# Head-pair loads and a folded row maximum at the start of a fused attention and feed-forward kernel

## The chip, the cores and the metric

One core of a Trainium2 chip. The metric is the device time of one execution in microseconds (us), median of several; the span in a profile, first to last instruction, is about 1.8 us shorter. Runs agree within some 0.5%, so a difference under 1 us in one pair of runs says little.

In the profiles PE is TensorE, PEld its weight loads, DVE VectorE, ACT ScalarE, POOL GpSimd and SPq SyncE's queue. SBUF is the core's on-chip memory; an eviction copies a matmul's result into SBUF; to issue a DMA is to hand it to the DMA engines, and it lands when its data has arrived.

## The reference, cut to what matters

Linear attention with random features (8 batches, 8 heads, 576 rows, 64 dimensions, 128 features), then a two-layer network (512 to 2048 to 512) on its 4608 rows:

```python
def phi(x):                        # x: q or k, scaled
    proj = np.einsum('bhsd,md->bhsm', x, omega)
    h = proj - np.sum(x * x, axis=-1, keepdims=True) / 2.0
    h = h - np.max(h, axis=-1, keepdims=True)      # row maximum over 128 features
    return np.exp(h) / np.sqrt(m)
kv  = np.einsum('bhsm,bhsd->bhmd', k_p, v);  z = np.sum(k_p, axis=2)
num = np.einsum('bhsm,bhmd->bhsd', q_p, kv); den = ... z ... + 1e-06
# x = num/den, heads side by side;  h = x @ w_in;  g = h*clip(h+3,0,6)/6;  return g @ w_out
```

In k's features the square term cancels against the maximum. The kernel takes the exponential first and then divides by the row maximum of the result, which it folds into v.

## The kernel before

A small scheduler in the program orders instructions and picks engines from estimated costs. Only batch 0 and 1 matter here. Cut to the parts concerned (cuts marked with `# ...`):

```python
# batch 0: k, q, v: one head of two head pairs per DMA (256 KB)
for x, (m0, m1) in enumerate(halves):            # [(0, 2), (2, 4)]
    for hh in range(2):
        # ...
        rows = src[b, 2 * m0 + hh:2 * m1 - 1 + hh:2, first:first + MAIN, :]
        dma("%s%d%d" % (t, hh, x), d[:, m0:m1, hh, :], rows.rearrange(...), 131072 * (m1 - m0), ...)
# ... cast to bf16 (kb), TensorE transposes, eviction (kT), projection, exponential (kp); nine units u:
op("DVE", dvet(512), lambda E, u=u: E.reduce_max(
    mx[pb][:, 4 * u:4 * u + 4], kp[pb][:, 4 * u:4 * u + 4, :], axis=AX.X), ...)
# reciprocals cc = 1/mx, then v scaled by them, on GpSimd (POOL) or VectorE (DVE):
op(EV_V if b else V0, {"POOL": 0.62, "DVE": dvet(260)}, lambda E, ...: E.tensor_tensor(
    vcl[pb][p0:p0 + 64, :, ...], vl[pb][p0:p0 + 64, :, :], <cc broadcast>, ALU.mult), ...)   # leftover rows
op(EV_V if b else V0, {"POOL": 1.2, "DVE": dvet(512)}, lambda E: E.tensor_tensor(
    vcm[:, :, 0:D], v32[:, m, :, :], cbc, ALU.mult), ...)                                     # vc of pair m
# TensorE: kv product of pair m: eight 65-wide matmuls kp x vc and one kp x vcl
```

The four kv products of batch 0 are the gate: before them TensorE has little to do, after them it hardly waits again.

The softmax here doesn't subtract the row's maximum and nothing guards it: scores larger than these inputs give would overflow.

Of the kernel before, what the change touches and what calls it, by code (L numbers as in the profile page):

```python
# [5 lines left out]
BF16 = mybir.dt.bfloat16  # L6
# [5 lines left out]

URGENT = 0.8
FIT = 0.05
IDLE_UNTIL = 21.0
# [27 lines left out]
class Prog:  # L43
# [60 lines left out]
    def schedule(self):  # L104
# [68 lines left out]
        while len(order) < n:  # L173
            best = None
            for e, lst in engines.items():
                cand = []
                for o in lst:
                    s = slot_of(o) if o.alloc else (0.0, ())
                    if s is None:
                        continue  # L180
                    cand.append((max(free[e], ready(o), s[0]), o, s[1]))
                if not cand:
                    continue
                idle = [x for x in cand if x[1].name == "idle"]
                cand = [x for x in cand if x[1].name != "idle"]
                m = min([x[0] for x in cand] + [1e9])
                if idle and (not cand or idle[0][0] + (0.02 if idle[0][0] < 8.0 else idle[0][1].occ) <= m):
                    if idle[0][0] > IDLE_UNTIL:
                        if not cand:
                            continue  # L190
                    elif best is None or idle[0][0] < best[0]:
                        best = (idle[0][0], e, idle[0][1], idle[0][2])
                        continue
                    else:
                        continue
                if not cand:
                    continue
                c = min((x for x in cand if x[0] <= m + (URGENT if x[1].prio < -1.0 else 0.02)),
                        key=lambda x: (x[1].prio, x[1].seq))
                fits = [x for x in cand if x[0] + (x[1].occ[e] if isinstance(x[1].occ, dict) else x[1].occ) <= c[0] + FIT]  # L200
                if c[0] > m + 0.02 and fits:
                    c = min(fits, key=lambda x: (x[1].prio, x[1].seq))
                if best is None or c[0] < best[0]:
                    best = (c[0], e, c[1], c[2])
# [7 lines left out]
            o.eng = e  # L212
            occ = o.occ[e] if isinstance(o.occ, dict) else o.occ
            for vx, i in zip(o.alloc, picks):
                old = vx.ring.held[i]
                if old is not None:
                    for d in old.users:
                        o.deps.setdefault(d, False)
                vx.slot = i
                vx.ring.held[i] = vx  # L220
# [98 lines left out]
def _emit(nc, es, q, k, v, omega, w_in, w_out, out):  # L319
# [13 lines left out]
    TU = [(0, 2), (2, 6), (6, 10), (10, 14), (14, 18)]  # L333
    HALVES = [(0, 2), (2, 4)]
    SPLIT = 3
    LATE = 0.4
    FIRST = [("k", 1), ("k", 0), ("q", 1), ("v", 0), ("v", 1), ("q", 0)]
    REST = [("k", 1), ("k", 0), ("q", 1), ("q", 0), ("v", 0), ("v", 1)]
    W_GATE = [("vl", 0)]*2+[("v32", 1, 3)]*2
    alpha = float(D) ** -0.25  # L340
    PE_T, PE_X = 2, 2
    SPARE = 1
    IDLE = (16, 60)
    EV_T = ("DVE", "ACT")
# [25 lines left out]
    kp = [sbt("kp%d" % u, [128, NCH, M], BF16) for u in range(2)]  # L370
    mx = [sbt("mx%d" % u, [128, NCH], F32) for u in range(2)]
    cc = [sbt("cc%d" % u, [128, NCH], F32) for u in range(2)]
    vc = [sbt("vc%d" % u, [128, 520], BF16) for u in range(2)]
# [34 lines left out]
    def dvet(n):  # L408
        return 0.07 + n / 960.0
# [64 lines left out]
    def w_in_piece(i, gate):  # L474
        f0, f1 = WI[i]
        op("POOL", 0.72 * (f1 - f0), lambda E: E.dma_start(
            wi[:, :, 128 * f0:128 * f1], w_in[:, 128 * f0:128 * f1].rearrange("(c p) f -> p c f", p=128)),
# [3 lines left out]
    def w_out_piece(g, gate):  # L481
        op("POOL", 2.95, lambda E: E.dma_start(
            wo[:, 4 * g:4 * g + 4, :], w_out[512 * g:512 * g + 512, :].rearrange("(c p) e -> p c e", p=128)),
# [7 lines left out]
    def load(b, eng, gates):  # L491
        pb = b % 2
        halves = HALVES if b == 0 else [(0, NP)]
        turn_of = [0]

        def dma(part, dst, src, n, keys, gate, prio, run):
            cast = b > 0 and part[0] in "kq"
            e = "POOL" if cast else eng[turn_of[0]] if turn_of[0] < len(eng) else "SP"
            op(e, n * (0.74 if b == 0 else 0.8) * (1.0 if run == 1024 else 1.5) / 262144.0,
               lambda E: E.dma_start(dst, src), prio + 0.001 * turn_of[0], reads=gate + (free if cast else []), writes=keys,  # L500
# [15 lines left out]
        def mains(t, src, dst):  # L516
            for x, (m0, m1) in enumerate(halves):
                for hh in range(2):
                    first = 64 * hh if t != "q" else 0
                    d = dst[:].rearrange("p m (h r) d -> p m h (r d)", h=2) if t == "v" else mains_of(dst)  # L520
                    rows = src[b, 2 * m0 + hh:2 * m1 - 1 + hh:2, first:first + MAIN, :]
                    dma("%s%d%d" % (t, hh, x), d[:, m0:m1, hh, :], rows.rearrange("m (p r) d -> p m (r d)", r=4),
                        131072 * (m1 - m0), landing(t, hh, m0, m1), gates[t], base[t], 1024)

# [20 lines left out]
    def attention(b):  # L545
# [19 lines left out]

        def four(m0, m1, hh):
            return [2 + 4 * m + 2 * hh + s for m in range(m0, m1) for s in range(2)]

        def every(m0, m1, s):
# [20 lines left out]

        def dbls(t):
            return t[:, 2:, :].rearrange("p (m h s) t -> p m h (s t)", h=2, s=2)

        def alts(t, s, m0, m1):
# [8 lines left out]
        if b == 0:  # L603
            for m0, m1 in HALVES:
                for hh in range(2):
                    nm = "%d%d" % (m0 // 2, hh)
                    dbl = four(m0, m1, hh)
                    cast("k", nm, 512, mains_of(kb)[:, m0:m1, hh, :], mains_of(k32)[:, m0:m1, hh, :],
                         main_keys("k", range(m0, m1), [hh]), dbl, 0)
                    turns("k", nm, dbl, dbls(kT)[:, m0:m1, hh, :], kb, 0)  # L610
            for s in range(2):
# [22 lines left out]
        for u in range(NU):  # L634
            vK = Virt(ring)

            def e_K(E, u=u, vK=vK):
# [9 lines left out]
               pos(u) + 0.02, reads=[vK], writes=[("kp", pb, u)], name="eK%d.%d" % (b, u))  # L647
            op("DVE", dvet(512), lambda E, u=u: E.reduce_max(  # L648
                mx[pb][:, 4 * u:4 * u + 4], kp[pb][:, 4 * u:4 * u + 4, :], axis=AX.X),
               pos(u) + 0.03, reads=[("kp", pb, u)], writes=[("mx", pb, u)], name="mx%d.%d" % (b, u))  # L650

# [25 lines left out]
        for hh in range(2):  # L677
            p0 = 64 * hh
            op(EV_V if b else V0, {"POOL": 0.62, "DVE": dvet(260)}, lambda E, hh=hh, p0=p0: E.tensor_tensor(  # L679
                vcl[pb][p0:p0 + 64, :, 65 * hh:65 * hh + 65], vl[pb][p0:p0 + 64, :, :],  # L680
# [57 lines left out]
    def pair(b, m, t):  # L738
# [10 lines left out]
        vcm = vc[u2][:].rearrange("p (c e) -> p c e", e=65)  # L749
        op(EV_V if b else V0, {"POOL": 1.2, "DVE": dvet(512)}, lambda E: E.tensor_tensor(  # L750
            vcm[:, :, 0:D], v32[:, m, :, :], cbc, ALU.mult),
# [263 lines left out]
```

## Time and profile before

| | before |
|---|---|
| time, median | 323.59 us (323.52 to 324.55) |
| span of the profiled run | 321.8 us |
| last kv product of batch 0 | 17.61 us |
| first second-layer matmul | 39.98 us |

```profile
12.33 1.43 POOL L679 TENSOR_TENSOR vcl<-vl,cc 64x260 bf16<-64x260 f32 x2
16.20 1.36 POOL L750 TENSOR_TENSOR vc<-v,cc 128x512 bf16<-128x512 f32 x1
```

While GpSimd multiplies vcl, VectorE does maxima; they last as long as elsewhere (five take 3.05 us in a row). While GpSimd multiplies vc, VectorE is already in its own vc, which it began 0.34 us sooner; VectorE's takes 0.80 us (its two others 0.70 and 0.69), GpSimd's 1.36, beside a median of 1.05 over its 22.

### The profile page before, as it was taken

The page shows a single profiled execution, that of the slowest core. Times are in us where ns is not written, and L with a number is a line of the kernel's source. Part 1 is how long each engine was busy: PE and PEld are TensorE (multiplying, and loading weights), DVE is VectorE, ACT ScalarE, POOL GpSimd, SP SyncE. Part 2 cuts the span into 40 slices and gives each one's busy share as a digit, 9 for nine tenths or more (in the row PEclk, how much of TensorE's full clock was granted, in tenths as well). Part 3 has the DMA queues.
Part 4 walks back from the last instruction along what each step waited for, and adds up shares of the span by engine and source line. Part 5 has one row for each costly group of instructions (what it writes and reads, how often), then busy time and mean ns, then how long its engine had stood idle before and what let it go on. Part 6 is the DMA issues. An engine that isn't in the chain of part 4 may idle for free.

```text
span 321.8 us, 5873 instructions
## 1 busy us (share of the span) xinstructions
PE 317.0 (98%) x2236; PEld 174.8 (54%) x2236; DVE 209.0 (65%) x460; ACT 189.1 (59%) x385; POOL 76.8 (24%) x107
## 2 busy tenths in 40 slices
PE   8999999999999999999999999999999999999996
PEld 6789855455654544565555545555555444444443
DVE  4988985597787947995796478846866353433411
ACT  3996982596595516966775387647674254344400
POOL 2765171065040600730333022402020000000000
DMA  7999999999940999897829963998012201000024
GB/s 249 269 201 204 236 146 234 225 184 170 226 122 34 136 173 271 99 196 118 236 31 188 191 208 39 183 201 224 16 50 67 73 27 41 33 35 33 33 67 98
DMA packets 91532, 44.79 MB, mean 139 GB/s; under 512 B 58096, under 2 KB 87024, under 8 KB 91504
## 3 DMA queue, kind: packets, MB, share of 16 engines
q1 hardware_dynamic: 64288, 31.31, 42.1%
q0 software_dynamic: 26512, 12.46, 31.4%
q10 hardware_dynamic: 704, 0.66, 0.6%
q8 instruction: 18, 0.29, 0.4%
q14 instruction: 10, 0.08, 0.1%
HBM read 36.73 MB, written 9.44 MB: 143 GB/s over the span
## 4 chain that ended last, share of the span: by engine, by line
PE 94%; DVE 4%; POOL 1%; issue 0%; ACT 0%; POOLq 0%; DVEq 0%
PE p L917 39%; PE p L859 34%; PE p L656 5%; PE p L639 4%; PE p L884 4%; PE p L791 3%; PE p L763 2%; DVE mx L648 2%; PE p L466 2%; PE p L429 1%; PE p L765 1%; POOL vc L750 0%; DVE vc L750 0%; DVE vcl L679 0%; DVE gT L895 0%
## 5 line engine op out<-in xcount | busy, mean ns | idle before, releaser
L917 PE MATMUL p<-wo,gT 128*128 128x512 bf16 (+2 forms) x592 | 141.0, 373 | 0.3 <-DVE qT L418 0.3
L867 DVE SCALAR_TENSOR_TENSOR gT<-tsb,p 128x512 bf16<-128x512 bf16 x128 | 86.8, 685 | 56.7 <-ACT tsb L865 56.1
L865 ACT ACTIVATE tsb<-p 128x512 bf16<-128x512 f32 x128 | 76.3, 601 | 71.1 <-PE p L859 70.6
L859 PE MATMUL p<-xT,wi 128*128 128x512 bf16 x448 | 107.3, 379 | 0.0
L917 PEld LDWEIGHTS p<-wo,gT 128*128 128x128 bf16 x592 | 56.1, 98 | 57.5 <-DVE qT L418 0.5
L859 PEld LDWEIGHTS p<-xT,wi 128*128 128x128 bf16 x448 | 42.6, 98 | 45.4
L648 DVE TENSOR_REDUCE mx<-kp 128x4 f32<-128x512 bf16 x72 | 46.7, 674 | 9.7 <-ACT kp L645 9.4
L645 ACT ACTIVATE kp<-p 128x512 bf16<-128x512 f32 x72 | 40.0, 619 | 15.1 <-PE p L639 15.1
L660 ACT ACTIVATE qpT<-p 128x512 bf16<-128x512 f32 (+1 forms) x80 | 41.4, 575 | 4.8 <-PE p L656 4.6
L750 POOL TENSOR_TENSOR vc<-v,cc 128x512 bf16<-128x512 f32 x22 | 23.4, 1064 | 36.3 <-DVE cc L746 27.0
L807 DVE TENSOR_TENSOR xb<-p,rec 128x384 bf16<-128x384 f32 (+1 forms) x64 | 28.5, 477 | 0.0
L639 PE MATMUL p<-om,kT 128*128 128x256 bf16 x144 | 23.0, 273 | 0.0
L656 PE MATMUL p<-qT,om 128*128 128x512 bf16 (+1 forms) x80 | 22.8, 358 | 0.0
L418 DVE COPY osb<-p 128x512 f32<-128x512 f32 (+2 forms) x12 | 7.8, 647 | 22.7 <-PE p L917 22.7
L417 ACT COPY osb<-p 128x512 f32<-128x512 f32 x25 | 14.8, 591 | 11.3 <-PE p L917 11.3
L500 POOL DMA_DIRECT2D k<-in_k_dram x12 | 9.1, 767 | 41.9 <-PE p L859 33.7
L639 PEld LDWEIGHTS p<-om,kT 128*128 128x128 bf16 x144 | 13.8, 98 | 9.7
L791 PEld LDWEIGHTS p<-kvz,qpT 128*128 128x128 bf16 x312 | 13.5, 98 | 5.8 <-ACT qpT L660 0.2
L859 PE MATMUL p<-xS,wi 128*128 128x512 bf16 x64 | 16.4, 379 | 0.0
L884 PE MATMUL p<-xT,wi 128*128 128x256 bf16 x128 | 15.9, 272 | 0.0
L763 PEld LDWEIGHTS p<-vc,kp 128*128 128x128 bf16 x256 | 11.9, 98 | 6.1 <-POOL vc L750 0.4
L791 PE MATMUL p<-kvz,qpT 128*128 128x65 bf16 x312 | 14.8, 194 | 0.0
(69 smaller groups left out, 215.9 us busy)
## 6 DMA issues: line engine op xcount, KB each, us to landing
out_dram<-osb SPq DMA_DIRECT2D x32, 256.0 KB, 2.6
v<-in_v_dram SPq DMA_DIRECT2D x14, 512.0 KB, 5.3
wi<-in_moe_w_in_dram POOLq DMA_DIRECT2D x4, 512.0 KB, 8.3
k<-in_k_dram POOLq DMA_DIRECT2D x8, 256.0 KB, 5.1
k<-in_q_dram POOLq DMA_DIRECT2D x8, 256.0 KB, 6.2
wo<-in_moe_w_out_dram POOLq DMA_DIRECT2D x4, 512.0 KB, 12.8
kb<-in_k_dram POOLq DMA_DIRECT2D x6, 256.0 KB, 5.3
qb<-in_q_dram POOLq DMA_DIRECT2D x6, 256.0 KB, 7.6
```

What stands on the lines that cost most here:

```text
L639: ins = E.matmul(ring.t[vK.slot][:, 256 * i:256 * i + 256], kT[:, 2 * u + i, :], om[:].rearrange("d t m -> d (t m)"), start=True, stop=True)
L645: op("ACT", actt(512), lambda E, u=u, vK=vK: E.activation(kp[pb][:, 4 * u:4 * u + 4, :].rearrange("p c m -> p (c m)"), ring.t[vK.slot], AF ...
L648: op("DVE", dvet(512), lambda E, u=u: E.reduce_max(mx[pb][:, 4 * u:4 * u + 4], kp[pb][:, 4 * u:4 * u + 4, :], axis=AX.X), pos(u) + 0.03, r ...
L656: op("PE", mmt(n), lambda E, vQ=vQ, lh=lh: E.matmul(ring.t[vQ.slot][:, 0:n], om[:, lh, :], src, start=True, stop=True), p + 0.045 * lh, re ...
L660: op("ACT", actt(n), lambda E, vQ=vQ, lh=lh: E.activation(dst(lh), ring.t[vQ.slot][:, 0:n].rearrange("m (j t) -> m j t", t=128), AF.Exp, s ...
L791: ins = E.matmul(d[:, hh, i - i0, :], qpT[pb][:, o:o + 128], kvz[m][:, 65 * hh:65 * hh + 65], start=True, stop=True)
L807: op("DVE", dvet(128 * n), lambda E: E.tensor_tensor(xv(i0, i1), psum()[:, :, :, 0:64], rbc, ALU.mult), t + 0.01, reads=[vn, ("rec", ru)], ...
L859: ins = E.matmul(ring.t[vh.slot], wi[:, c, 128 * f:128 * f + 128], xv[:, c, :], start=(c == 0), stop=(c == NJ - 1))
L865: op("ACT", actt(512), lambda E: E.activation(tsb[tu][:], ring.t[vh.slot], AF.Relu, bias=0.5, scale=1.0 / 6.0), t - 0.1, reads=[vh], write ...
L867: op("DVE", dvet(512), lambda E: E.scalar_tensor_tensor(gT[gu][:, f, :], tsb[tu][:], 1.0, ring.t[vh.slot], ALU.min, ALU.mult), t - 0.1, re ...
L884: ins = E.matmul(ring.t[vh.slot][:, 256 * g:256 * g + 256], wi[:, c, 128 * (f + g):128 * (f + g) + 128], xT[0][:, c, 256 * half:256 * half ...
L917: ins = E.matmul(ring.t[vo.slot][:, 0:c1 - c0], gT[gu][:, f, 128 * tc:128 * tc + 128], wo[:, f, c0:c1], start=(f == 0), stop=(f == NF - 1))
```

## The change

It is meant to bring the first bytes of k in sooner, so that the first batch's chain starts sooner, and to shorten the row maximum: a bf16 elementwise maximum of the features' two halves (the fold), then a maximum over 64. Scheduler constants and costs are adjusted with it, so order and engines change too. The core of the diff (cut):

```diff
-URGENT = 0.8
-FIT = 0.05
+COLD = 6.0
+URGENT = 0.5
+FIT = 0.1
...
+    PARTS = {"k": [(0, 1, 0, 1), (0, 1, 1, 2)] + [(1, 2, 0, 1), (1, 2, 1, 2)] + [(m, m + 1, 0, 2) for m in range(2, NP)],
+             "q": [(0, 2, 0, 1), (0, 2, 1, 2), (2, 4, 0, 1), (2, 4, 1, 2)],
+             "v": [(m, m + 1, 0, 2) for m in range(NP)]}
...
-    W_GATE = [("vl", 0)]*2+[("v32", 1, 3)]*2
+    W_GATE = [("q32", 1, 3)] * 2 + [("v32", 0, 1)] * 2
+    FOLD = 2
...
-            op("DVE", dvet(512), lambda E, u=u: E.reduce_max(
-                mx[pb][:, 4 * u:4 * u + 4], kp[pb][:, 4 * u:4 * u + 4, :], axis=AX.X),
+            if b >= FOLD:
+                ...                                     # as before
+            op("DVE", 0.07 + 256 / 1920.0, lambda E, u=u, fu=fu: E.tensor_tensor(
+                fold[fu][:], kp[pb][:, 4 * u:4 * u + 4, 0:64], kp[pb][:, 4 * u:4 * u + 4, 64:128], ALU.max), ...)
+            op("DVE", dvet(256), lambda E, u=u, fu=fu: E.reduce_max(
+                mx[pb][:, 4 * u:4 * u + 4], fold[fu][:], axis=AX.X), ...)
...
-        op(EV_V if b else V0, {"POOL": 1.2, "DVE": dvet(512)}, lambda E: E.tensor_tensor(
+        op(EV_V if b else V0, {"POOL": 1.32, "DVE": dvet(512)}, lambda E: E.tensor_tensor(
```

k's main rows now come in six DMAs (four of 128 KB, two of 256 KB) in place of four, with the leftover rows in one more.

More of the change, by code (lines that the diff above doesn't have):

```diff
@@ L186, in schedule @@
                 m = min([x[0] for x in cand] + [1e9])
-                if idle and (not cand or idle[0][0] + (0.02 if idle[0][0] < 8.0 else idle[0][1].occ) <= m):
+                if idle and (not cand or idle[0][0] + (0.02 if idle[0][0] < 4.8 else 0.2 if idle[0][0] < 8.0 else idle[0][1].occ) <= m):
                     if idle[0][0] > IDLE_UNTIL:
@@ L213, in schedule @@
             occ = o.occ[e] if isinstance(o.occ, dict) else o.occ
+            if e == "PE" and 4.0 < st < COLD:
+                occ *= 2.0
             for vx, i in zip(o.alloc, picks):
@@ L334, in _emit @@
     HALVES = [(0, 2), (2, 4)]
+    PARTS = {"k": [(0, 1, 0, 1), (0, 1, 1, 2)] + [(1, 2, 0, 1), (1, 2, 1, 2)] + [(m, m + 1, 0, 2) for m in range(2, NP)],
+             "q": [(0, 2, 0, 1), (0, 2, 1, 2), (2, 4, 0, 1), (2, 4, 1, 2)],
+             "v": [(m, m + 1, 0, 2) for m in range(NP)]}
+    KPARTS = [(m, h0, h1) for m, _, h0, h1 in PARTS["k"]]
     SPLIT = 3
@@ L371, in _emit @@
     mx = [sbt("mx%d" % u, [128, NCH], F32) for u in range(2)]
+    fold = [sbt("fold%d" % u, [128, 4, 64], BF16) for u in range(3)]
     cc = [sbt("cc%d" % u, [128, NCH], F32) for u in range(2)]
@@ L475, in w_in_piece @@
         f0, f1 = WI[i]
-        op("POOL", 0.72 * (f1 - f0), lambda E: E.dma_start(
+        op("POOL", 0.64 * (f1 - f0), lambda E: E.dma_start(
             wi[:, :, 128 * f0:128 * f1], w_in[:, 128 * f0:128 * f1].rearrange("(c p) f -> p c f", p=128)),
@@ L481, in w_out_piece @@
     def w_out_piece(g, gate):
-        op("POOL", 2.95, lambda E: E.dma_start(
+        op("POOL", 2.56, lambda E: E.dma_start(
             wo[:, 4 * g:4 * g + 4, :], w_out[512 * g:512 * g + 512, :].rearrange("(c p) e -> p c e", p=128)),
@@ L492, in load @@
         pb = b % 2
-        halves = HALVES if b == 0 else [(0, NP)]
         turn_of = [0]
@@ L498, in dma @@
             e = "POOL" if cast else eng[turn_of[0]] if turn_of[0] < len(eng) else "SP"
-            op(e, n * (0.74 if b == 0 else 0.8) * (1.0 if run == 1024 else 1.5) / 262144.0,
+            op(e, n * 0.74 * (1.0 if run == 1024 else 1.5) / 262144.0,
                lambda E: E.dma_start(dst, src), prio + 0.001 * turn_of[0], reads=gate + (free if cast else []), writes=keys,
@@ L516, in mains @@
         def mains(t, src, dst):
-            for x, (m0, m1) in enumerate(halves):
-                for hh in range(2):
-                    first = 64 * hh if t != "q" else 0
-                    d = dst[:].rearrange("p m (h r) d -> p m h (r d)", h=2) if t == "v" else mains_of(dst)
-                    rows = src[b, 2 * m0 + hh:2 * m1 - 1 + hh:2, first:first + MAIN, :]
-                    dma("%s%d%d" % (t, hh, x), d[:, m0:m1, hh, :], rows.rearrange("m (p r) d -> p m (r d)", r=4),
-                        131072 * (m1 - m0), landing(t, hh, m0, m1), gates[t], base[t], 1024)
+            for m0, m1, h0, h1 in PARTS[t] if b == 0 else [(0, NP, 0, 1), (0, NP, 1, 2)]:
+                off = 64 if t != "q" else 0
+                d = dst[:].rearrange("p m (h r) d -> p m h (r d)", h=2) if t == "v" else mains_of(dst)
+                rows = bass.AP(src.tensor, src.offset + ((b * H + 2 * m0 + h0) * S + off * h0) * D,
+                               [[4 * D, 128], [2 * S * D, m1 - m0], [(S + off) * D, h1 - h0], [1, 4 * D]])
+                dma("%s%d%d" % (t, m0, h0), d[:, m0:m1, h0:h1, :], rows, 131072 * (m1 - m0) * (h1 - h0),
+                    [x for hh in range(h0, h1) for x in landing(t, hh, m0, m1)], gates[t], base[t], 1024)
         def lefts_of(t, hh):
@@ L564, in rows_of @@
             return [k_ for x in dbl for k_ in ([(t + "b", pb, x, h) for h in hs] if x < 2 else [(t + "b", pb, x)])]
-        def four(m0, m1, hh):
-            return [2 + 4 * m + 2 * hh + s for m in range(m0, m1) for s in range(2)]
         def every(m0, m1, s):
@@ L589, in turns @@
                p, reads=[vT], writes=[(t + "T", x) for x in dbl], name="Tev%s%d.%s" % (t, b, name))
-        def dbls(t):
-            return t[:, 2:, :].rearrange("p (m h s) t -> p m h (s t)", h=2, s=2)
         def alts(t, s, m0, m1):
@@ L603, in attention @@
         if b == 0:
-            for m0, m1 in HALVES:
-                for hh in range(2):
-                    nm = "%d%d" % (m0 // 2, hh)
-                    dbl = four(m0, m1, hh)
-                    cast("k", nm, 512, mains_of(kb)[:, m0:m1, hh, :], mains_of(k32)[:, m0:m1, hh, :],
-                         main_keys("k", range(m0, m1), [hh]), dbl, 0)
-                    turns("k", nm, dbl, dbls(kT)[:, m0:m1, hh, :], kb, 0)
+            for m, h0, h1 in KPARTS:
+                nm = "%d%d" % (m, h0)
+                dbl = [2 + 4 * m + x for x in range(2 * h0, 2 * h1)]
+                cast("k", nm, 256 * (h1 - h0), mains_of(kb)[:, m, h0:h1, :], mains_of(k32)[:, m, h0:h1, :],
+                     main_keys("k", [m], range(h0, h1)), dbl, 0)
+                turns("k", nm, dbl, kT[:, dbl[0]:dbl[-1] + 1, :], kb, 0)
             for s in range(2):
@@ L647, in attention @@
                pos(u) + 0.02, reads=[vK], writes=[("kp", pb, u)], name="eK%d.%d" % (b, u))
-            op("DVE", dvet(512), lambda E, u=u: E.reduce_max(
-                mx[pb][:, 4 * u:4 * u + 4], kp[pb][:, 4 * u:4 * u + 4, :], axis=AX.X),
-               pos(u) + 0.03, reads=[("kp", pb, u)], writes=[("mx", pb, u)], name="mx%d.%d" % (b, u))
+            if b >= FOLD:
+                op("DVE", dvet(512), lambda E, u=u: E.reduce_max(
+                    mx[pb][:, 4 * u:4 * u + 4], kp[pb][:, 4 * u:4 * u + 4, :], axis=AX.X),
+                   pos(u) + 0.03, reads=[("kp", pb, u)], writes=[("mx", pb, u)], name="mx%d.%d" % (b, u))
+                continue
+            fu = u % 3
+            op("DVE", 0.07 + 256 / 1920.0, lambda E, u=u, fu=fu: E.tensor_tensor(
+                fold[fu][:], kp[pb][:, 4 * u:4 * u + 4, 0:64], kp[pb][:, 4 * u:4 * u + 4, 64:128], ALU.max),
+               pos(u) + 0.03, reads=[("kp", pb, u)], writes=[("fold", fu)], name="fold%d.%d" % (b, u))
+            op("DVE", dvet(256), lambda E, u=u, fu=fu: E.reduce_max(
+                mx[pb][:, 4 * u:4 * u + 4], fold[fu][:], axis=AX.X),
+               pos(u) + 0.03, reads=[("fold", fu)], writes=[("mx", pb, u)], name="mx%d.%d" % (b, u))
         def project(name, dbl, src, dst, p):
@@ L678, in attention @@
             p0 = 64 * hh
-            op(EV_V if b else V0, {"POOL": 0.62, "DVE": dvet(260)}, lambda E, hh=hh, p0=p0: E.tensor_tensor(
+            op(EV_V if b else V0, {"POOL": 0.72, "DVE": dvet(260)}, lambda E, hh=hh, p0=p0: E.tensor_tensor(
                 vcl[pb][p0:p0 + 64, :, 65 * hh:65 * hh + 65], vl[pb][p0:p0 + 64, :, :],
```

## The prediction

> **What bounds the kernel now.** I read the page first (busy shares, then the chain that ended last), then the chain in order of time for the first 45 us, then the timeline and busy time by stretch there, and last the waits.
>
> ```profile
> PE 317.0 (98%) x2236; PEld 174.8 (54%) x2236; DVE 209.0 (65%) x460; ACT 189.1 (59%) x385; POOL 76.8 (24%) x107
> ...
> PE 94%; DVE 4%; POOL 1%; issue 0%; ACT 0%; POOLq 0%; DVEq 0%
> ```
>
> TensorE carries 94% of the chain and is busy 98%. That busy share flatters it, since matmul ends are modelled, so I add up issue intervals instead. Runs of one form in the chain of waits give the interval: 42 matmuls of 256 columns in 4.59 us are 109 ns each, 40 of 512 columns in 8.63 us are 216 ns, and eight of 65 columns in 0.25 us are 31 ns. With the counts in the groups by form this makes 1136 x 216 ns = 245.0 us (512 columns), 288 x 109 = 31.4 (256), 576 x 31 = 17.9 (65), 120 transposes and the like at 56 = 6.7, and 4.4 for the 130 and 384 wide ones: 305.4 us of work that the change does not touch. The span is 321.8, so only 16.4 us are overhead. They are 1.3 us before the first matmul, about 3.0 after the last one (it ends near 318.8), 8.9 of filler matmuls, and 3.2 of true gaps. By stretch, the counts fill 60 to 290 us completely; the gaps lie in the first 40 us. There the chain is not TensorE alone:
>
> ```profile
> 1.32 2.74 PE p L466 x12
> ...
> 4.17 1.28 PE p L466 x6
> ...
> 8.05 0.65 DVE kT L418 x2
> 8.70 2.96 DVE mx L648 x5
> ...
> 11.91 0.68 DVE vc L750
> 12.59 1.19 DVE mx L648 x2
> 13.77 0.60 DVE vc L750
> 14.37 1.08 DVE mx L648 x2
> ...
> 16.20 1.37 POOL vc L750
> 17.57 0.05 issue
> 17.61 0.43 PE p L763 x8
> ```
>
> The columns are start, length and what. L466 is filler[...]. From 8.05 to 16.2 us VectorE paces the first batch: kT evictions, nine row maxima (L648), reciprocals and the scaling of v (vc). Then GpSimd scales the last v, and at 17.61 the last kv product goes out. From there on TensorE leads the chain, until batch 1 comes:
>
> ```profile
> 35.35 0.69 DVE gT L895
> 36.04 1.85 DVE mx L648 x4
> ...
> 38.62 0.87 DVE vcl L679
> ...
> 39.50 0.43 DVE qT L418
> ```
>
> Here TensorE truly waits again: of the 22.4 us from 17.6 to 40, counts times intervals account for 21.5, so 0.9 us is lost. These two places, the start and the 0.9 us, are all that the change can touch. The stretch view shows why arrival matters at the start:
>
> ```profile
> 2.00:4.00 2.00, 2.00 (x12) 1.44 (x11) 0.50 (x5) 1.22 (x2) 0.00 (x0) 1.00 0.94 319
> 4.00:6.00 2.00, 2.00 (x14) 1.51 (x13) 0.67 (x3) 1.06 (x2) 0.61 (x1) 1.00 1.04 315
> 10.00:12.00 2.00, 2.00 (x23) 1.69 (x21) 2.00 (x7) 2.00 (x6) 1.38 (x2) 1.00 1.11 347
> ```
>
> After stretch and length, the columns are busy time (count) of TensorE, its weight loads, VectorE, ScalarE and GpSimd, then clock, DMA share and GB/s. DMA is full from 2 us on; VectorE is idle until 6 us and full from 8 to 16.
>
> [...] 12 fillers in 2.74 us are 228 ns each, against 109 later. [...]
>
> **The change, part by part.**
>
> First loads. In the before kernel the first k casts start at 3.82 (ScalarE), 4.73 (GpSimd), 5.25 and 6.28 us, each on a 256 KB transfer that holds one head of two pairs. 256 KB at 320 GB/s is 0.82 us. After, the first four are 128 KB, so each lands about 0.4 us after its forerunner. I put the first pieces at 3.2 to 3.5 us, the fourth near 4.4, all of k near 6.3 as before (same bytes). The first exponential of k waited until 7.35 because four transposes of a whole 512-wide piece stood before it. In the built order of the changed kernel, eight transposes of 256-wide pieces and then the first projections stand there. VectorE's omega copies end at 4.79 as now; four 256-wide evictions at 0.28 us end at 5.9, so the exponentials can begin near 6. The later k pieces still gate the rest. Before its first fold VectorE also has the cast of the k leftovers (landing near 6.7, 0.28 us), a 512-wide eviction (0.42) and a 256-wide one (0.28), so it gets to the maxima at about 7.7 in place of 8.70: 1.0 us gained.
>
> Row maximum. For nine units: before 9 x 592 = 5.33 us. [...] The later batches keep the old maximum and lie where TensorE is full. [...]
>
> What moves. On VectorE one vc (about 0.65) goes to GpSimd, two vcl (64x260, about 0.33 each) come from GpSimd, and one qT eviction (0.42) comes from ScalarE: some 0.4 us more. Start 1.0 [...] - 0.4 = 1.2 us earlier at the last kv product, 16.4 in place of 17.61. GpSimd's second vc (1.37) could end a little later than that, but it starts sooner too, as the weight loads in front of it are issued sooner.
>
> TensorE order. Before the last kv product the changed kernel has six 512-wide q projections, the old one four: 2 x 216 ns = 0.43 us of work are pulled into the waiting time. Sum: 1.2 + 0.43 = 1.6 us.
>
> Cross-check by fillers. The built order has 52 in place of 63: three fewer at the cold rate (3 x 213 ns = 0.64) and eight fewer warm (8 x 109 = 0.87), 1.5 us less dead work. Two independent counts agree.
>
> Batch 1. [...] of the 0.9 us lost there I credit 0.2, since ScalarE is as full there (4.00 of 4 us between 36 and 40) and eight exponentials take 4.0 us. Against it: the loads of w_out do not hurry. DMA is full until 44 us and the first piece lands at 28.0 + 10.4 = 38.4, while the first second-layer matmul ran at 39.98; pulled forward by 1.6 it would meet the landing. I take 0.2 back. The new scheduling constants reorder later instructions too, but TensorE is full there: 0.
>
> Expected: 323.6 - 1.6 = 322.0 us, half a per cent.
>
> **The rivals.**
>
> A. The reorder only reveals another limit: DMA, full from 2 to 44 us. If v, the w_in pieces or w_out land when they landed before, TensorE waits on them and the gain shrinks to some 0.3 to 0.8 us (322.8 to 323.3). For it: the DMA share, and SyncE waiting 18.5 us on w_out. Against: the third and fourth w_out pieces now arrive 2 to 3 us before use, and w_in's gate moves from the v leftovers to a q piece that was issued earlier.
>
> B. The clock. Six early cold fillers become three, and the new rule for fillers leaves short gaps between 4.8 and 8 us unfilled. [...] 30 to 60 early matmuls run at half rate. That costs at most 3 us, but mostly inside time that waits for VectorE anyway; the result would be 322.5 to 325.
>
> C. More than I see: if VectorE's early idle time is really used up and batch 1's 0.9 us vanishes too, 2.5 to 3 us go, 320.6 to 321.
>
> D. A new stall mid-kernel from the changed scheduling (URGENT 0.5, FIT 0.1). One wait of a microsecond there would eat the gain, for TensorE has no slack there.
>
> **Range and chances.** The centre is 322.0. Four parts in five lie between C's best and a nearly lost gain, 320.8 to 323.3. Faster by 2% would need 6.5 us out of 16.4 of overhead, of which 4.3 are fixed ends and 7.4 are fillers that remain in the program's order: 1%. Slower by 2% needs 6.5 us of new waits, B and D together: 2%.
>
> **What would show it.** Right: the first exponential of k starts near 6 instead of 7.35; [...] the last of the four kv products is at 16 to 16.7; the filler group counts 52; the stretches from 60 to 290 us hold the same matmuls as before, only shifted by 1 to 2 us. Wrong: [...] matmuls of 256 columns at 213 ns after 6 us; a wait of TensorE on a DMA of w_in or w_out near 20 or 38 us; gaps between 60 and 300 us. If the kv product comes earlier but the first second-layer matmul still starts near 39.9, rival A holds.

What it said of the hardware without a measurement is cut, and with it what rested on that alone: the lengths of the fold and of the shorter maximum, and so the gain of the row maximum, one term of the sum. With that term the sum came to 1.2 us at the last kv product and to 1.6 us in all; the terms that are left, 1.0 and - 0.4, make 0.6 of the 1.2. The 592 ns of a maximum before come from its trace: five in a row take 2.96 us in the chain. The 0.33 of a vcl is an estimate: VectorE's shortest there is recorded with 426 ns, and a vc recorded with 0.69 us takes 0.60 in the chain. L466's fillers multiply constants while TensorE waits. The 512-wide matmuls of this trace are recorded with 379 ns on average, though they step by 216.

## More of the kernel before

In the timeline of SyncE's queue (start us, length us, engine, line, operation, tile, count) the line is a group of DMA issues; this is the time of issuing, not of transfer:

```profile
1.21 1.45 SPq L500 DMA_DIRECT2D k<-in_k_dram  x3
```

Three issues of k take 1.45 us, so k's last is out at 2.66. (ScalarE's queue issues two more of k meanwhile.) In the timelines of VectorE and of GpSimd, two pairs of lines overlap in time:

```profile
12.50 1.27 DVE L648 TENSOR_REDUCE mx<-kp 128x4 f32<-128x512 bf16 x2
15.86 0.80 DVE L750 TENSOR_TENSOR vc<-v,cc 128x512 bf16<-128x512 f32 x1
```

## The result, and the profile after

| | before | after |
|---|---|---|
| time, median (same rounds) | 323.77 us (323.52 to 325.13) | 324.58 us (324.02 to 325.29) |
| ratio | | 1.002, 95% interval 0.9996 to 1.0043 |
| span of the profiled run | 321.8 us | 322.6 us |
| first exponential of k | 7.35 us | 6.55 us |
| last kv product of batch 0 | 17.61 us | 19.32 us |
| first second-layer matmul | 39.98 us | 41.00 us |

A ratio here is the mean time of one kernel's fast runs over that of the other's in the same rounds, so it is not quite the ratio of the medians. No gain came, and the result is outside the predicted range. The traces show that the start became 1.7 us slower where 1.2 us were to be gained.

The page of the changed kernel, engines and chain:

```profile
PE 314.2 (97%) x2190; PEld 173.5 (54%) x2225; DVE 212.8 (66%) x489; ACT 187.5 (58%) x378; POOL 75.7 (23%) x107
...
PE 90%; DVE 4%; ACT 2%; DMA 1%; issue 1%; SPq 1%; DVEq 0%
```

TensorE's share of the chain fell from 94 to 90%. Its chain of waits at the start (start, length, what):

```profile
3.12 4.65 DMA k<-in_k_dram
...
7.80 0.38 DVE kb L427
...
8.84 0.40 DVE fold L655 x2
9.24 0.33 DVE mx L658
...
10.22 0.53 DVE fold L655
...
14.07 1.19 DVE vcl L689
...
15.70 0.80 DVE fold L655 x2
...
17.69 1.27 DVE vc L760
19.00 0.43 PE p L773 x8
```

Before, the chain up to 8 us was TensorE; now it hangs on a transfer of k until 7.77. The first two folds take 0.40 us, 0.20 each, but a single fold takes 0.53 at 10.22 and two take 0.80 at 15.70. The last vc takes 1.27 us, beside 0.60 and 0.68 for those of before. Two readings suggest themselves.

The first is in SyncE's queue:

```profile
1.20 2.39 SPq L508 DMA_DIRECT2D k<-in_k_dram  x5
```

Each issue takes 0.42 to 0.47 us, for 128 KB as for 256 KB. Two more of them put k's last issue 0.93 us later than before (3.59 beside 2.66), and the issues of q and v behind it wait as long. The windows tell the same by rate (after stretch and length: busy time and count of TensorE, weight loads, VectorE, ScalarE, GpSimd, then clock, DMA share, GB/s):

```profile
4.00:6.00 2.00, 2.00 (x16) 1.69 (x15) 1.59 (x6) 0.32 (x1) 0.64 (x3) 1.00 0.95 235
```

That is 235 GB/s in a stretch that had 315 before, although the DMA share is still 0.95. The last pair of k reaches its cast at 7.41 in place of 6.28.

The second is in the timelines of VectorE and GpSimd:

```profile
13.69 1.56 DVE L689 TENSOR_TENSOR vcl<-vl,cc 64x260 bf16<-64x260 f32 x2
15.62 0.89 DVE L655 TENSOR_TENSOR fold<-kp 128x256 bf16<-128x256 bf16 x2
17.60 1.34 DVE L760 TENSOR_TENSOR vc<-v,cc 128x512 bf16<-128x512 f32 x1
```

```profile
14.99 1.16 POOL L760 TENSOR_TENSOR vc<-v,cc 128x512 bf16<-128x512 f32 x1
17.35 1.05 POOL L760 TENSOR_TENSOR vc<-v,cc 128x512 bf16<-128x512 f32 x1 [1.20 <-DVE cc L756]
```

Each VectorE instruction that lasts too long reads two tiles of SBUF, and a GpSimd instruction lies beside it: its casts of q (9.32 to 10.61) beside the fold at 10.22, its vc beside the others (beside the vcl pair only for the last 0.26 us, by the records; before that GpSimd issues DMAs). The prediction had not reckoned with this. The vc product, the vcl product and the fold have two SBUF inputs. The maximum that the fold replaces has one, and in the kernel before it lasted as long beside GpSimd's vcl as elsewhere (two take 1.27 us at 12.50, beside it, and at 14.29).

So the theory had two parts: **P**, contention with GpSimd's casts and products, makes VectorE's folds and products longer; and **L**, k's tail comes late because of its DMA issues. The rivals: **N**, the instructions are simply longer than estimated, whatever GpSimd does; **W**, VectorE is simply overloaded with the moved work and no contention is at play, so more work on it makes the product later. The runs show that instructions become longer, and not by what.

### The profile page after: what moved, and what is told of

It reads as the page before. It is cut to its first block, busy times and chain, and to the rows that moved or that the text cites. A ratio compares the mean times of both kernels' runs of the same rounds, so it can differ in the third digit from the quotient of the medians.

```text
span 322.6 us, 5819 instructions
## 1 busy us (share of the span) xinstructions
PE 314.2 (97%) x2190; PEld 173.5 (54%) x2225; DVE 212.8 (66%) x489; ACT 187.5 (58%) x378; POOL 75.7 (23%) x107
## 4 chain that ended last, share of the span: by engine, by line
PE 90%; DVE 4%; ACT 2%; DMA 1%; issue 1%; SPq 1%; DVEq 0%
PE p L927 37%; PE p L869 33%; PE p L894 4%; PE p L640 4%; PE p L666 3%; PE p L801 3%; PE p L773 2%; ACT qpT L670 2%; DMA k<-in_k_dram 1%; PE p L438 1%; DVE fold L655 1%; DVE mx L658 1%; DVE vc L760 1%; SPq L508 1%; PE p L775 0%
## 5 line engine op out<-in xcount | busy, mean ns | idle before, releaser
L927 PE MATMUL p<-wo,gT 128*128 128x512 bf16 (+2 forms) x576 | 139.1, 374 | 0.8
L650 DVE TENSOR_REDUCE mx<-kp 128x4 f32<-128x512 bf16 x54 | 36.0, 677 | 17.0 <-ACT kp L646 16.6
L760 POOL TENSOR_TENSOR vc<-v,cc 128x512 bf16<-128x512 f32 x21 | 22.2, 1059 | 46.7 <-DVE cc L756 31.8
L640 PE MATMUL p<-om,kT 128*128 128x256 bf16 x144 | 23.7, 277 | 0.1
L427 DVE COPY osb<-p 128x512 f32<-128x512 f32 (+2 forms) x11 | 7.1, 643 | 17.8 <-PE p L927 17.8
L773 PE MATMUL p<-vc,kp 128*128 128x65 bf16 x256 | 13.3, 195 | 1.3 <-DVE vcl L689 0.7
```

What stands on the lines that cost most here:

```text
L640: ins = E.matmul(ring.t[vK.slot][:, 256 * i:256 * i + 256], kT[:, 2 * u + i, :], om[:].rearrange("d t m -> d (t m)"), start=True, stop=True)
L650: op("DVE", dvet(512), lambda E, u=u: E.reduce_max(mx[pb][:, 4 * u:4 * u + 4], kp[pb][:, 4 * u:4 * u + 4, :], axis=AX.X), pos(u) + 0.03, r ...
L773: E.matmul(o[:, 65 * hh:65 * hh + 65], kp[pb][:, c0 + i, :], vc[u2][:, 65 * i:65 * i + 65], start=(i == 0), stop=False)
L927: ins = E.matmul(ring.t[vo.slot][:, 0:c1 - c0], gT[gu][:, f, 128 * tc:128 * tc + 128], wo[:, f, c0:c1], start=(f == 0), stop=(f == NF - 1))
```

## The experiments

Kernels of the first letter "a" are the changed kernel with an edit made after the scheduling, so that order stays; those with "b" are the kernel before, likewise, except where said. Each ratio is to the kernel before in the same rounds; its median there was 323.77 us (a_single_max, a_kl_act, b_fold), 323.84 (a_vc_dve, b_parts, b_sched, a_m3_act), 324.28 (b_fold0, b_vc_dve, b_fold0_vc_dve) and 323.85 (a_kl_vc). The edits shown are cut or abridged. Each place is read from one profiled execution; the landings of the same DMAs differ by 0.2 to 0.4 us between executions, so smaller shifts prove nothing.

**1. m_ports: the durations by themselves.** In place of the whole kernel (wrong result), VectorE repeats folds, maxima, vcl and vc products on constant tiles, four times over: alone, and while GpSimd runs products (ptt), casts (pcast) or DMA issues (pdma).

```diff
+ for ph in ("alone", "ptt", "pcast", "pdma"):
+     # GpSimd: 24 x tensor_tensor 128x512 | 24 x cast 128x512 | 24 x dma_start | nothing
+     for rep in range(3):
+         # VectorE: 4 folds, 4 maxima of 256, 4 maxima of 512, 2 vcl, 2 vc
```

> A measurement by itself, wrong result on purpose. VectorE runs the disputed forms (fold 4x64 bf16, maximum over 256 and over 512, 64x260 and 128x512 f32 products with a broadcast column) first alone, then beside GpSimd products, GpSimd casts, and GpSimd DMA issues. Theory P [...]: alone the fold steps in about 0.2 us, beside GpSimd products 0.5 us or more on average, the two maxima stay at 0.33 and 0.59 us in all phases, the f32 products rise from about 0.35 and 0.6 us to 0.8 and more. Rival N (no contention, the slow instances in the changed kernel come from something else): all forms alike in all four phases, within 10%.

The groups by form (line, engine, operation, tiles, shapes, count | busy us, mean ns | idle before):

```profile
L373 DVE TENSOR_TENSOR fptt<-kp 128x256 bf16<-128x256 bf16 x12 | 7.7, 703 | 0.0
L373 DVE TENSOR_TENSOR fpcast<-kp 128x256 bf16<-128x256 bf16 x12 | 5.1, 487 | 0.0
L373 DVE TENSOR_TENSOR falone<-kp 128x256 bf16<-128x256 bf16 x12 | 2.7, 285 | 0.0
L373 DVE TENSOR_TENSOR fpdma<-kp 128x256 bf16<-128x256 bf16 x12 | 2.7, 285 | 0.0
L377 DVE TENSOR_REDUCE m256ptt<-fptt 128x4 f32<-128x256 bf16 x12 | 4.2, 412 | 0.1
```

A fold takes 285 ns alone and 703 beside GpSimd's products; beside casts 487, beside DMA issues 285. The maximum doesn't notice (411 alone, 412 beside products; that over 512: 675 and 676). The vc product goes from 689 to 1216, vcl from 418 to 884. This is P; N falls. The records of successive instructions overlap: 12 folds, recorded with 285 ns, fill 2.7 us of busy time, 225 ns each.

**2. a_single_max: the changed kernel with the old maximum in the fold's place.**

```diff
- E.tensor_tensor(fold[fu][:], kp[..., 0:64], kp[..., 64:128], ALU.max);  E.reduce_max(mx[...], fold[fu][:])
+ E.reduce_max(mx[pb][:, 4 * u:4 * u + 4], kp[pb][:, 4 * u:4 * u + 4, :], axis=AX.X)   # at the maximum's place
```

> The changed kernel in its own instruction order, but each fold deleted and its second maximum again taken over all 512 elements. In the changed kernel nine folds and nine short maxima of batch 0 took about 2.5 + 3.0 = 5.5 us of VectorE's time, against 9 x 0.59 = 5.3 us for nine full maxima. Theory P (folds that overlap GpSimd eat the gain): last kv product within 0.3 us of the changed kernel's 19.3, time within 0.3 us of it (324.3 to 324.9). Rival F (the fold is a plain gain of 0.5 us, the loss is elsewhere): last kv product 0.5 us later, time 325.1.

Ratio 1.0022 (0.9992 to 1.0053), fast runs 323.44, 324.88 and 325.52 us: the same as with the fold (1.002). In this order the fold gives nothing that the times can show. The three fast times span the forecasts of P and of F, so this run decides nothing between them. The profiled run was slow (clock 0.657), so its places are not read.

**3. a_kl_act: the DMA of k's leftovers issued by ScalarE's queue.** In the changed kernel 0.43 us of issue stand beside a 128 KB transfer, which at 315 GB/s (the rate before in this stretch) also takes 0.42 us: not small.

```diff
+    for o in G.order:
+        if o.name == "kl.0":
+            o.eng = "ACT"
```

> The changed kernel in its own order, but the transfer of the k leftovers is issued from ScalarE's queue as its third, not from SyncE's as its fifth. Theory L (the leftovers land at 7.80 us because they stand behind five transfers, and VectorE and TensorE, which take them in order, stand still until then): they land near 6 us, the first fold comes at 7.9 to 8.2 in place of 8.84, the last kv product 0.6 to 0.9 us sooner, time 323.7 to 324.0. Theory P alone: the first folds come sooner, but the chain is made up later by GpSimd overlap, and the last kv product moves by less than 0.3 us, time 324.3 to 324.7.

The leftovers' cast ran at 6.56 in place of 7.80, the first fold at 8.11 in place of 8.76, the last kv product at 18.86 in place of 19.32. So L is a part of the loss, by 0.46 us in this profile (L had said 0.6 to 0.9, P alone under 0.3); run 12, with the same loads, did not repeat it. The fourth pair of k, whose issue had kept its place (2.61 us), landed at 7.30 and was cast at 7.42, as in the changed kernel. The time did not follow: ratio 1.0049 (0.9999 to 1.01), four runs between 323.95 and 327.47 us; the profiled one, 324.28, had a span of 322.5 us.

**4. a_m3_act: the DMA of k's fourth pair issued by ScalarE's queue instead.** The edit is that of 3 with `"k30.0"`.

> The changed kernel in its own order, but the fourth pair of k (256 KB) is issued from ScalarE's queue as its third transfer, so that SyncE carries 512 KB of k and the leftovers, and ScalarE 512 KB, as before. Theory L2 (one queue alone brings k home slower: 194 GB/s between 4 and 5 us against 311): the rate between 4 and 6 us rises above 280 GB/s, the fourth pair lands near 6.4 in place of 7.4 and the leftovers near 7.0 in place of 7.8, the first fold comes near 8.0 in place of 8.84, last kv product 0.5 us sooner. Rival D (the 16 engines are full anyway): rate and landings within 0.3 us of the changed kernel.

The profiled run was slow (clock 0.753), but transfers can be read with care: 307 GB/s from 4 to 6 us in place of 235 (run 3 had 303). SyncE's issues of k ended at 3.08 there. So the rate does come back with one issue fewer on the queue. The pair itself, issued at 1.67 in place of 2.61, landed at 6.39 in place of 7.29, as L2 had said. That did not help: GpSimd casts the third pair first, which now landed at 6.81 in place of 5.80, so the cast of the fourth began only near 7.55; the leftovers landed at 7.35 in place of 7.77. The time was worse, not better: 1.0059 (1.0042 to 1.0075), 325.57 to 325.91 us. L predicted the rate and the landing of the pair, and missed the rest and the time.

**5. b_parts: the kernel before with the new loads alone,** scheduled anew (the two hunks with PARTS and KPARTS, nothing else).

> The kernel before with the split loads of batch 0 alone (the casts and transposes of k follow the new pieces), scheduled anew with the old constants and the old maximum. Theory L (the split makes the tail of k land later: 7.4 and 7.8 us in place of 6.3 and about 7): the last piece of k lands after 7 us, the first exponential comes sooner (6.0 to 6.6), but the last kv product not before 17.6, time 323.6 to 324.6. My prediction's step: the last kv product 1 us sooner, 16.6, time 322.8.

Ratio 1.0021 (1.0006 to 1.0036), last kv product at 18.32 in place of 17.61. The first exponential came sooner, at 5.59, but k's last pieces reached their casts at 7.42 and 8.00, and SyncE's queue shows the same 2.39 us for five issues. The DMA engines moved 199 GB/s from 4 to 6 us. The smaller loads alone lose 0.7 us of start: the opposite of the gain of 1.0 that the prediction gave them.

**6. b_sched: the kernel before with the new scheduler constants and costs alone.**

> The kernel before with the scheduler's constants and operation costs of the changed kernel alone: old loads, old maximum. The built order puts one vcl on VectorE and one fewer vcl on GpSimd in batch 0. Theory P: VectorE's two-input products overlap more with GpSimd, the last kv product comes at 17.8 to 18.5, time 323.8 to 324.8. Rival Z (the constants are neutral): last kv product 17.4 to 17.8, time within 0.3 us of 323.7.

Ratio 1.0006 (0.999 to 1.0023), 324.17 us, but the last kv product at 19.21, later than either theory said. GpSimd's vc began at 17.12, VectorE's at 17.19, and the latter took 1.51 us. The first second-layer matmul came at 40.76: 1.60 us lost at the product are 0.78 there. The new order has six 512-wide q projections in front of the product in place of four, which softens the delay.

**7. b_fold: the kernel before with the fold in batches 0 and 1,** each fold put right ahead of its maximum, order kept.

```diff
+    for o in G.order:
+        if o.name.startswith("mx0.") or o.name.startswith("mx1."):
+            # F: fold of this unit, inserted here; o now reduces fold[u % 3] over 64
```

> The kernel before in its own order, with each of the 18 full maxima of batches 0 and 1 replaced by a fold and a short maximum in its place. Rival F (plain gain): VectorE's nine maxima of batch 0 take 4.7 in place of 5.3 us, the last kv product moves from 17.6 to about 17.2, time 323.3 (ratio 0.9985). Theory P: folds beside GpSimd's casts, vcl and vc take 0.5 us or more, the nine pairs take 5.3 us or more, the last kv product stays at 17.5 to 18.0, time 323.6 to 324.2.

Ratio 1.0068 (1.005 to 1.0086), fast runs 325.45 to 326.49 us: a clear loss, larger than P had said (323.6 to 324.2).

**8. b_fold0: the fold in batch 0 only** (the condition cut to `"mx0."`).

> The kernel before in its own order with the fold in batch 0 alone (the run with the fold in batches 0 and 1 lost 0.7%, and its profile fell in the slow state). Theory P: the nine shorter maxima let VectorE's third vc start at the same moment as GpSimd's, both are long (1.5 us on VectorE), the last kv product comes at 18.5 to 19.2 in place of 17.6, time 324.4 to 325.6. Rival Q (the loss of that run came from batch 1): last kv product at 17.0 to 17.6, time 323.2 to 323.8.

Ratio 1.0063 (1.0041 to 1.0085), 326.07 us; a fast profile with a span of 323.2 (its run, 325.02 us, is the fastest of the six, so the others lost more than it shows). Last kv product at 19.02, 1.41 us later than before; first second-layer matmul 1.40 later; span 1.4 longer. The place is where P had put it (18.5 to 19.2), the time is above P's 324.4 to 325.6. All of the profile's loss is at the start, 1.21 us of it before VectorE's third vc (17.07 in place of 15.86). VectorE's timeline:

```profile
10.09 0.29 DVE L988 TENSOR_TENSOR fold<-kp 128x256 bf16<-128x256 bf16 x1
10.41 0.42 DVE L990 TENSOR_REDUCE mx<-fold 128x4 f32<-128x256 bf16 x1
10.75 0.28 DVE L988 TENSOR_TENSOR fold<-kp 128x256 bf16<-128x256 bf16 x1
...
11.80 1.08 DVE L751 TENSOR_TENSOR vc<-v,cc 128x512 bf16<-128x512 f32 x1
12.81 0.70 DVE L988 TENSOR_TENSOR fold<-kp 128x256 bf16<-128x256 bf16 x1
...
17.07 1.56 DVE L751 TENSOR_TENSOR vc<-v,cc 128x512 bf16<-128x512 f32 x1
```

Two things are to be seen. First, with nothing of GpSimd's beside it but DMA issues, fold plus maximum is a step of 0.66 us (10.09 to 10.75), more than the single maximum's 0.59. The maximum reads what the fold has just written, so it starts 0.32 us after the fold's start, not 0.20 as an independent successor does (in the changed kernel's chain, 13.45 to 13.65). Second, the fold at 12.81 lies in GpSimd's vcl pair (12.23 to 14.05) and takes 0.70 us; in the kernel before, maxima stood beside that pair. (Another fold, at 15.83, takes 0.52 us beside a cast of GpSimd's.) The vc ahead of it is recorded with 1.08 us, though it began before the first vcl; with a maximum behind it, as in run 9, it takes 0.77, so a part of the fold's wait may be booked on it (argued, not shown). And at 17.05 GpSimd's vc began 0.02 us before VectorE's, which took 1.56.

**9. b_vc_dve: the kernel before with GpSimd's vc of batch 0 on VectorE.**

```diff
+    for o in G.order:
+        if o.name.startswith("vc.0."):
+            o.eng = "DVE"
```

> The kernel before in its own order, with the one vc that GpSimd made in batch 0 (1.37 us, the last thing before the last kv product) put on VectorE. Theory P: VectorE's third vc falls from 0.80 to 0.69 us, the fourth follows at once, last kv product 17.0 to 17.3 in place of 17.6, time 323.2 to 323.6. Rival W (VectorE is the bound, added work delays): 17.8 to 18.2, time 324.0 to 324.4.

Ratio 1.0008 (0.9982 to 1.0033), 324.03 us; last kv product at 18.09, 0.48 later, span 0.5 longer. P had expected a gain here and missed; the numbers lie where W had put them. But most of the 0.48 is not the edit's: in this execution the second piece of v landed at 12.17 in place of 11.80, and VectorE's first vc began 0.37 us later (12.26 in place of 11.89), its third 0.35 later (16.21 in place of 15.86). From there to the last product it took 1.88 us in place of 1.75. So the edit cost some 0.1 us, within what landings alone can do, and gained nothing: in the kernel before VectorE starts its vc first and loses little (0.80 us), and GpSimd, whose vc is lengthened, ends at 17.56; on one engine the two stand one after the other (0.70 and 0.72 us in the chain, the last ending at 17.72), and the third product waits for the second of them. Set beside run 8, where GpSimd was 0.02 us ahead, contention is a matter of the moment, not of the pairing.

**10. b_fold0_vc_dve: both edits.**

> Both: the fold in batch 0 and all vc of batch 0 on VectorE. Theory P says that the fold is a gain of about 0.5 us as soon as GpSimd multiplies nothing beside it (GpSimd's two vcl at 12.3 to 13.8 still cost one or two folds 0.4 us each): last kv product 16.6 to 17.1, time 322.8 to 323.3, faster than the kernel before by 0.1 to 0.3%. Rival F2 (the fold and second maximum is never shorter than one maximum in this place): last kv product at or after that of the run without fold.

Ratio 1.0063 (1.0039 to 1.0087), 326.35 us, last kv product at 18.93. P missed again, and F2's forecast held (a later product than in 9, without the fold): the last two vc are free of contention (0.70 and 0.66 us; 1.75 us from the third vc to the last product, as in the kernel before), but the steps of fold and maximum and the contention with GpSimd's vcl (vc 1.10, fold 0.70) are as in 8. So the fold's loss in the old order is mostly not GpSimd's vc: 1.32 us are lost before the third vc (17.18 in place of 15.86). By the lengths of 8, vcl accounts for 0.8 of it, four dependent steps for 0.3 and a cast beside a fold for 0.2; that no other wait hides in this sum is argued, not shown.

**11. a_vc_dve: the changed kernel with GpSimd's vc of batch 0 on VectorE** (the edit of 9).

> The changed kernel in its own order, but both products vc that GpSimd made in batch 0 are put on VectorE, the busier engine of the two. Theory P ([...]measured alone, a fold takes 285 ns and 703 beside GpSimd products, a 64x260 product 418 and 884, a 128x512 product 689 and 1216): VectorE gets two more products of 0.6 us, but its own vcl, folds and vc between 13.7 and 19 us fall back to 0.4, 0.28 and 0.69 us, and the last kv product goes out at 18.0 to 18.6 in place of 19.3. Rival W (VectorE is simply overloaded with moved work[...]): it goes out 0.6 to 1.2 us later, 19.9 to 20.5. In time 0.5 us less or 0.8 us more than the changed kernel.

Last kv product at 18.17 in place of 19.32, of which 0.25 came from an earlier landing of k in that run. Time 323.98 us, ratio 1.0009 (0.9981 to 1.0037), span 321.4. VectorE's timeline answers the lines of the changed kernel one by one:

```profile
9.87 0.28 DVE L655 TENSOR_TENSOR fold<-kp 128x256 bf16<-128x256 bf16 x1
...
13.10 0.81 DVE L689 TENSOR_TENSOR vcl<-vl,cc 64x260 bf16<-64x260 f32 x2
...
14.88 0.49 DVE L655 TENSOR_TENSOR fold<-kp 128x256 bf16<-128x256 bf16 x2
...
17.11 0.68 DVE L760 TENSOR_TENSOR vc<-v,cc 128x512 bf16<-128x512 f32 x1
```

The vcl pair takes 0.81 in place of 1.56, two folds 0.49 in place of 0.89, the last vc 0.68 in place of 1.34. GpSimd's DMA issues still lie beside vcl (13.18 to 14.70), so they were not what had lengthened it. VectorE got two more products to do and finished sooner. P holds in this order, and W falls. How much the edit is worth is less clear: of the 1.15 us, 0.25 is the landing, and 0.33 the fold at 9.87, which here began 0.16 us ahead of GpSimd's second cast of q and took 0.28 us, while in the changed kernel it met that cast (0.61). That is contention too, but it fell away by the moment and not by the edit. Some 0.55 us are left for taking GpSimd's vc off.

**12. a_kl_vc: the edits of 3 and 11 together.**

> The changed kernel, order kept, with two repairs together: the four leftover rows of k issued by ScalarE's queue (alone it brought the last kv product from 19.32 to 18.86) and both of GpSimd's value products of batch 0 on VectorE (alone 18.17, of which 0.25 was an earlier landing). Additive theory [...]: first fold near 8.1, no fold over 0.30 us alone, last kv product at 17.6 to 18.0, beside 17.61 in the kernel before; ratio to the kernel before 0.996 to 1.001, so at best its equal. Rival (the DMA issue on ScalarE costs what it gains, as its timed runs suggested, or a third cause is at work): last kv product later than 18.2, or a ratio of 1.002 to 1.006 in spite of an early last kv product.

Ratio 1.0001 (0.9987 to 1.0014), 323.95 us: equal to the kernel before, as the additive theory (L and P together make the whole loss) had it; a_vc_dve alone (1.0009, 0.9981 to 1.0037) can't be told from it. But the profiled run (324.80 us, one of the two slowest of six) missed the places: k came late again, with the last two casts at 6.83 and 7.59, and the last kv product at 19.73, where the rival had said "later than 18.2". With the same loads the first fold came at 9.21 here and at 8.11 in run 3. The windows show why it fell so far behind:

```profile
6.00:8.00 2.00, 0.64 (x8) 0.44 (x7) 0.38 (x3) 1.08 (x2) 1.02 (x2) 0.94 1.07 370
8.00:10.00 2.00, 2.00 (x14) 1.57 (x13) 1.36 (x5) 0.60 (x1) 1.13 (x3) 0.50 1.14 323
```

TensorE was busy for only 0.64 of 2 us while it waited for k, and then its granted clock was 0.50; six 256-wide projections took 1.29 us, 215 ns each. This is the prediction's rival B, in one run of one kernel. So the additive theory agrees with the times and is not supported by a place.

The places of all fast profiles, as differences from the kernel before:

| kernel | last kv product | first second-layer matmul | span |
|---|---|---|---|
| b_vc_dve | +0.48 | +0.47 | +0.5 |
| b_fold0 | +1.41 | +1.40 | +1.4 |
| b_fold0_vc_dve | +1.32 | +1.30 | +1.4 |
| b_parts | +0.71 | +0.73 | +0.8 |
| b_sched | +1.60 | +0.78 | +0.8 |
| changed kernel | +1.71 | +1.02 | +0.8 |
| a_kl_act | +1.25 | +0.34 | +0.7 |
| a_vc_dve | +0.56 | -0.35 | -0.4 |
| a_kl_vc | +2.12 | +1.21 | +1.2 |

In the old order a delay of the last kv product goes through to the end in full. In the order of the new constants some 0.7 to 0.9 us of it are made up by the first second-layer matmul, because more TensorE work stands ahead of the product: six 512-wide q projections in place of four are 0.43 us of it, the rest was not traced. That is why a start 1.7 us slower costs 0.8 us.

## Why the prediction was wrong

The step that failed is the sum of three terms (one is cut) that made the start, in its words, "1.2 us earlier at the last kv product, 16.4 in place of 17.61". It came at 19.32, 2.9 us off. None of the three gains or costs came as counted, each for a reason shown above.

- "All of k near 6.3 as before (same bytes)" and so "start 1.0". The first pieces landed as predicted (casts at 3.10, 3.76, 3.91 and 4.38) and the first exponential moved to 6.55, but the fourth pair landed at 7.29 (cast at 7.41) and the leftovers at 7.77 (cast at 7.80), where the kernel before had 6.16 and 6.70. The first fold began at 8.84 in the chain, where 7.7 was predicted: 1.14 us. The bytes are the same; the issues are not, and two more on one queue put the last of them 0.93 us later. k's last pieces land some 4.5 to 4.7 us after their issue in both kernels, and in a_m3_act the pair issued 0.94 us sooner landed 0.90 sooner. b_parts shows that the loads alone turn the gain into a loss.
- The gain of the row maximum (the term that is cut). Alone there is one: an uncontended fold in this order is a step of 0.20 us and its maximum 0.33, so nine of both would take 4.77 us in place of 9 x 592 ns = 5.33, 0.56 less. But nine folds took 2.53 us of the chain in place of 9 x 0.20 = 1.80, because GpSimd was casting or multiplying beside three of them (0.33 too much beside a cast, 0.40 beside a vc); the 0.73 eats the 0.56. Where a fold stands right ahead of its own maximum, the step is 0.66 even alone.
- "What moves": "some 0.4 us more". Two vcl came to VectorE and one vc went to GpSimd, priced at lone durations. The vcl pair took 1.48 us in the chain in place of the 0.66 estimated; without GpSimd's vc behind it (a_vc_dve) 0.81. The last vc took 1.27 in the chain, for GpSimd's had begun 0.25 us sooner; that is no longer than the vc of 1.37 on GpSimd that ended the stretch before.

Added up: in the kernel before, the stretch from the first maximum (8.70) to the last reciprocals (15.80) took 7.1 us. With the 0.56 of the lone steps and the 0.4 of what moves it would have taken 7.1 - 0.56 + 0.4 = 6.94; it took 8.57 (8.84 to 17.41). Of the 1.63 too much, vcl makes 0.82 and the folds 0.73; 0.08 are small differences. With the 1.14 of the late start that is 2.77 of the 2.92 us; the rest is 0.1 after the last reciprocals and what the cut term had been over the 0.56.

The other steps. The bound was right: between 60 and 290 us both kernels make the same 1512 weight loads. The rates of the fillers were read right (228 ns each for the first twelve, 109 later); what ends the slow rate is not shown. "0.43 us of work pulled into the waiting time" was right in kind: 0.69 us were made up between the kv product and the second layer. The fillers are 52, as counted, but the cross-check failed: fewer fillers meant not less lost time but open waits in their place, 0.67 us on vcl and 0.53 on vc, which the kernel before did not have. Rival A named a late transfer, but of other tensors and for bandwidth; TensorE waited on no weights. B did not occur in the changed kernel's profile, nor did D; that B's span (322.5 to 325) holds the measured 324.58 is luck. The range was too narrow because no rival had the start itself getting slower.

What stays open. a_kl_act and a_m3_act were timed slower than their places or rates suggest, and their runs scatter more than those of the kernel before; slow states took two of the profiles that could have told why. Why the third pair of k slipped by 1.0 us when the fourth was issued sooner (a_m3_act), and why the loads of a_kl_act came late again in a_kl_vc, was not found; that the number of issues, and not the smaller pieces as such, sets the rate rests on 303 and 307 GB/s in a_kl_act and a_m3_act. By the records, GpSimd's vc overlaps VectorE's second vcl by only 0.26 us (its times are rough), less than the vcl is lengthened; that the vc is its cause rests on a_vc_dve, and on a_m3_act, where the vc lies plainly beside the second vcl (14.59 to 15.70) and the pair takes the same 1.56 us. Also, the time of the changed kernel against the kernel before (1.002) is within the noise; that it isn't faster is shown, that it is slower is shown only by the places.

## What to carry to other kernels

A replacement that is faster alone must be priced with its inputs: beside GpSimd's products the fold, with two SBUF inputs, went from 285 ns to 703 (487 beside casts), while the maximum over 512 that it shortens, with one, stayed at 675 to 676. So what GpSimd does at that moment decides what the fold costs. Halving the first transfers doubles their issues, and where an issue takes as long as the transfer, as here (0.42 to 0.47 us beside 0.42 for 128 KB at 315 GB/s), the tail of the same tensor pays for its head. Before a place is put down to an edit, check that everything ahead of the edit came at the same time in both executions. A delay at the gate is worth what work the order holds in front of it: look at the same mark further down before calling it lost.
